# Splitting the 512-column matmuls of the second MLP's second product into two of 256 columns

## The chip, the cores and the metric

The kernel runs on one core of one Trainium2 chip. The metric is the device time of one execution in microseconds (us), as the median of several runs; smaller is better. Engines are named as in the profile: PE is TensorE's matmul, PEld its weight load (the stationary operand of a matmul), DVE is VectorE, ACT is ScalarE, POOL is GpSimd, and SP issues most DMAs.

## What is computed

Three layers follow one another. Linear attention with an RMS norm makes `x` of 2304 tokens by 512. A first MLP with three input products, a maximum over them and an output product follows. The second MLP, a mixture of four dense experts, takes more than half of the time, and the change is in it:

```python
def _moe2_ref(x, domain_probs, w1, w2):
    p = domain_probs / (domain_probs.sum(-1, keepdims=True) + 1e-09)
    out = np.zeros((2304, 512), dtype=np.float32)
    for e in range(4):
        h = np.maximum(x @ w1[e], 0.0)          # 512 -> 1024
        out += p[:, e:e + 1] * (h @ w2[e])      # 1024 -> 512
    return out
```

`h @ w2[e]` is the second product of the second MLP.

## The kernel before, in words

All matmuls of the MLPs use operands of type fp32r. To keep more precision, a value is split into a high part and a low remainder, and a product of two values is made of three matmuls: high by high, high by low, low by high. They are summed in a PSUM bank of 512 fp32 columns.

The second MLP works in rounds. A round (loop at L1029) is one expert `e` (4), one superblock `sb` of 768 tokens (3) and one `pr` (4), which stands for two blocks of 128 hidden channels: 48 rounds in all. Each round has two kinds of matmuls, written to different banks:

- The first product of this round. `seven` (L591) is called seven times (`k` = 0 to 6, through `product`, L586). Each call issues 6 matmuls of 384 columns (L597): seven products stand for the eight of a 2 by 2 block multiplication, by sums and differences of operands formed ahead. They alternate between two banks, 7 and 6. After each, ACT and DVE read the bank, form the hidden values and split them into high and low parts (L619 to L625, and `hide`, L603).
- The second product of the round before. `second` (L728) is a generator: for each of six blocks of 128 tokens (`ORDER`, banks 3, 4, 5, 0, 1, 2), for two blocks of hidden channels `a`, and for the three high and low pairs, it issues one matmul (L736). Its stationary operand is a 128 by 128 piece of the hidden values `h`, its moving operand is a row block of `w2` of 128 by 512. That makes 36 matmuls of 512 columns in a round and 1728 in 48 rounds.

The order on PE is written by hand. After the `k`-th product of the round the loop takes `AFTER[k]` matmuls from the generator (`AFTER` at L461, its sum is 36), so that PE has work while ACT and DVE read out the product's bank. When the last matmul of a token block in the last `pr` has been issued, the generator yields the block's number, and `store` (L746) scales the bank by the expert's probability, adds it up and writes it to memory. After the last round the loop at L1061 runs the 36 remaining matmuls with nothing between them.

The first MLP is run in the same manner, with matmuls of 384 columns only (L260, L424, L597, L704), before the first matmul of L736 at 376.2 us.

Of the kernel before, what the change touches and what calls it, by code (L numbers as in the profile page):

```python
# [21 lines left out]
def tile_attn_moe_moe2(  # L22
# [23 lines left out]
    nc = tc.nc  # L46
# [4 lines left out]
    P = 128  # L51
# [5 lines left out]
    TPB = T // P  # L57
# [21 lines left out]
    banks = [ps.tile([P, 512], F32, name=f"bank{n}") for n in range(8)]  # L79
# [372 lines left out]
    NPR = NEF // 2  # L452
# [5 lines left out]
    BANKS = "AXAXAAX"  # L458
    BEGIN = (0, 1, 3)

    AFTER = (5, 5, 5, 5, 7, 5, 4)  # L461


    FILL = [(0, 2, 1, 2, 2, 5, 2, 2), (0, 2, 1, 2, 2, 5, 2, 2), (0, 2, 1, 2, 2, 5, 2, 2)]
# [29 lines left out]
    def w_slot(pr):  # L494
        t, at = (wl, 0) if pr == 0 else (wr[0], (pr - 1) * 11 * DM)
        first = [part(t, at + i * 7 * 2 * P, 7 * 2 * P) for i in range(2)]
        at += 7 * DM
        second = [
            [part(wl, 11 * DM, DM) if (pr, a, i) == (3, 1, 1) else part(t, at + (2 * a + i) * DM, DM) for i in range(2)]
            for a in range(2)  # L500
        ]
        return first, second
# [76 lines left out]
    def y_split(k):  # L579
        hi, lo = y_op(k)  # L580
        src = y_part(Y_AT[k]).rearrange("p (c t) -> p c t", c=2)
        nc.scalar.activation(out=hi, in_=src, func=AF.Copy)  # L582
        low(lo, src, hi)
# [25 lines left out]
    def h_of(n):  # L609


        s = (2, 5) if n % 2 else (0, 1)
        return {(0, 0): h_unit(s[0]), (1, 0): h_unit(s[1]), (0, 1): h_unit(3), (1, 1): h_unit(4)}
# [114 lines left out]
    def second(n, pr):  # L728

        h = h_of(n + NPAIRS + 1)  # L730
        _, w = w_slot(pr)
        for i in ORDER:
            for a in range(2):
                for m, (hi, wi) in enumerate(((0, 0), (0, 1), (1, 0))):
                    last = (a, m) == (1, 2)
                    nc.tensor.matmul(  # L736
                        banks[i], h[a, i // TPB][hi][:, i % TPB * P : (i % TPB + 1) * P], w[a][wi],
                        start=(pr == 0 and a == 0 and m == 0), stop=(pr == NPR - 1 and last),
                    )
                    yield i if last else None  # L740

    def o_load(sb):
        for i in ORDER:
# [37 lines left out]
    with tc.manual_schedule():  # L781
# [75 lines left out]
        for st in steps:  # L857
# [33 lines left out]
            elif kind == "A":  # L891
                i, j, f = at
# [136 lines left out]
        for n, (e, sb, pr) in enumerate(rounds):  # L1029
# [3 lines left out]
            if before is not None:  # L1033
                e0, sb0, pr0 = before
                rest = second(n - 1, pr0)
            for k in range(7):
                product(pr, k)
                after_product(n, k)
                if n == 0:
                    lag_at(7 * len(units) + k)  # L1040
                    go(fill, FILL_18[1 + k])
                    for i in SPLIT.get((0, k), ()):
                        y_split(i)
                for _ in range(AFTER[k]):
                    ended = next(rest, None)
# [15 lines left out]
        for i in second(n, pr):  # L1061
            if i is not None:
                store(e, sb, i)
# [32 lines left out]
```

## Time and profile before

| what | value |
| --- | --- |
| median of 3 runs | 1129.35 us (1128.74 to 1131.17) |
| profiled execution, its time from first to last instruction (span) | 1126.5 us |
| PE busy | 1105.5 us, 98% of the span |
| PEld busy | 1014.4 us, 90% |
| DVE, ACT, POOL busy | 662.0, 429.0 and 156.4 us |

The profile records one execution. It gives no time of its own for that execution beside the span; the median of the runs is 2.85 us above the span. In the timeline a row is a merged run of equal instructions: its start, its length from the first start to the last end, engine, line, operation, the output and inputs by name, the shapes and the count. Matmuls overlap at their ends: the length of one matmul in a row is longer than the distance from its start to the next one's start. The distance between starts is the rate at which PE goes on, and it is got from the starts of two rows and the count of matmuls from the one to the other.

### The profile page before, as it was taken

What the parts mean: (1) busy time and instruction counts of PE and PEld (TensorE: products, weight loads), DVE (VectorE), ACT (ScalarE), POOL (GpSimd) and SP (SyncE); (2) the same over time, 40 slices, a digit from 0 to 9 for tenths busy, and PEclk for the clock granted to TensorE, in tenths of its full rate; (3) what the DMA queues carried; (4) which work ended last, traced back from release to release, by engine and by line L of the source; (5) the groups of instructions that cost most, each with busy time, mean ns of one, the idle gap of its engine ahead of it and who ended that gap; (6) DMA issues with size and microseconds to landing.
All of it is one profiled execution on the core that took longest, in us unless ns stands there. A gap on an engine that the chain in (4) does not pass through costs nothing.

```text
span 1126.5 us, 15294 instructions
## 1 busy us (share of the span) xinstructions
PE 1105.5 (98%) x6020; PEld 1014.4 (90%) x6020; DVE 662.0 (59%) x1023; ACT 429.0 (38%) x774; POOL 156.4 (14%) x164
## 2 busy tenths in 40 slices
PE   7899999999999999999999999999999999999998
PEld 7789999999999989988889988898989988898987
DVE  3889985667667672445745454764535575544523
ACT  2553233434344453343624242442324353323321
POOL 1346632420101100012100002110000220000000
PEclk8999999999999999999999999999999999999999
DMA  9955555332511503032230406240120625040111
GB/s 268 289 152 172 151 180 197 128 113 83 160 38 38 187 19 112 1 131 75 88 138 19 150 1 211 70 171 35 66 103 26 200 75 187 1 168 2 57 55 57
DMA packets 89257, 123.20 MB, mean 109 GB/s; under 512 B 11616, under 2 KB 57696, under 8 KB 89184
## 3 DMA queue, kind: packets, MB, share of 16 engines
q1 hardware_dynamic: 88480, 121.89, 33.8%
q8 instruction: 47, 0.77, 0.3%
q10 hardware_dynamic: 704, 0.33, 0.1%
q14 instruction: 26, 0.21, 0.1%
HBM read 87.59 MB, written 34.60 MB: 108 GB/s over the span
## 4 chain that ended last, share of the span: by engine, by line
PE 83%; DVE 9%; DMA 2%; issue 2%; ACT 1%; SPq 1%; POOL 1%; DVEq 0%; ACTq 0%; POOLq 0%
PE bank L597 42%; PE bank L736 36%; PE bank L704 3%; PE bank L424 1%; DVE cv_a L233 1%; DMA w_da<-cv_a 1%; DMA v<-in_v_dram 1%; DVE rb L508 1%; DVE fa L405 1%; DVE cv_a L236 1%; DMA k<-in_k_dram 1%; DVE cv_a L232 1%; DVE wr L210 1%; POOL cv_a L225 0%; SPq L138 0%
## 5 line engine op out<-in xcount | busy, mean ns | idle before, releaser
L736 PE MATMUL bank<-wr,hr 128*128 128x512 f32 x720 | 197.3, 393 | 0.0
L622 DVE TENSOR_TENSOR fa<-bank,fa 128x384 f32<-128x384 f32 x144 | 80.2, 557 | 181.3 <-ACT fa L619 99.6
L538 POOL TENSOR_TENSOR w1s<-w1s 128x256 f32<-128x256 f32 x96 | 82.7, 881 | 634.2 <-DMA w1s<-in_moe_w_dram 559.1
L597 PE MATMUL bank<-xr,wr 128*128 128x384 f32 x756 | 153.5, 338 | 0.0
L736 PEld LDWEIGHTS bank<-wr,hr 128*128 128x128 f32 x720 | 133.6, 188 | 17.8
L597 PEld LDWEIGHTS bank<-xr,wr 128*128 128x128 f32 x756 | 135.9, 188 | 9.8
L619 ACT ACTIVATE fa<-bank 128x384 f32<-128x384 f32 x144 | 70.5, 489 | 188.8 <-PE bank L597 188.0
L597 PE MATMUL bank<-rb,wr 128*128 128x384 f32 x696 | 141.3, 337 | 0.5 <-DVE hr L605 0.5
L597 PEld LDWEIGHTS bank<-rb,wr 128*128 128x128 f32 x696 | 125.1, 188 | 10.4 <-DVE hr L605 0.8
L736 PE MATMUL bank<-wl,hr 128*128 128x512 f32 x360 | 102.8, 394 | 0.0
L736 PE MATMUL bank<-wr,xr 128*128 128x512 f32 x288 | 93.9, 394 | 0.0
L597 PE MATMUL bank<-rb,wl 128*128 128x384 f32 x384 | 77.8, 339 | 0.1
L736 PEld LDWEIGHTS bank<-wl,hr 128*128 128x128 f32 x360 | 66.8, 188 | 8.6
L597 PEld LDWEIGHTS bank<-rb,wl 128*128 128x128 f32 x384 | 68.2, 188 | 4.2 <-DVE fa L680 0.4
L736 PE MATMUL bank<-wr,rb 128*128 128x512 f32 x216 | 69.0, 393 | 0.0
L605 DVE SCALAR_TENSOR_TENSOR hr<-fa,hr 128x384 fp32r<-128x384 f32 x72 | 43.4, 603 | 42.6 <-ACT hr L604 42.6
L604 ACT ACTIVATE hr<-fa 128x384 fp32r<-128x384 f32 x72 | 37.8, 525 | 78.8 <-DVE fa L622 78.8
L604 ACT ACTIVATE xr<-fa 128x384 fp32r<-128x384 f32 x48 | 25.2, 526 | 98.7 <-DVE fa L622 98.7
L736 PEld LDWEIGHTS bank<-wr,xr 128*128 128x128 f32 x288 | 53.9, 188 | 7.9
L680 DVE TENSOR_TENSOR fa<-bank,fa 128x384 f32<-128x384 f32 x54 | 29.9, 554 | 51.6 <-ACT fa L677 36.3
L508 DVE TENSOR_TENSOR rb<-fa,rb 128x768 fp32r<-128x768 f32 (+1 forms) x45 | 42.5, 946 | 28.8 <-ACT rb L582 28.1
L573 DVE TENSOR_TENSOR fa<-fa 128x768 f32<-128x768 f32 x56 | 54.4, 984 | 0.3
(175 smaller groups left out, 1759.7 us busy)
## 6 DMA issues: line engine op xcount, KB each, us to landing
fa<-y_d SPq DMA_DIRECT2D x24, 768.0 KB, 6.0
stage_a<-in_moe_w_dram SPq DMA_DIRECT2D x18, 512.0 KB, 3.9
o_d<-fa SPq DMA_DIRECT2D x36, 256.0 KB, 3.7
fa<-o_d SPq DMA_DIRECT2D x36, 256.0 KB, 5.3
w2s<-in_moe_w_dram SPq DMA_DIRECT2D x32, 256.0 KB, 3.7
w1s<-in_moe_w_dram SPq DMA_DIRECT2D x30, 256.0 KB, 2.9
w_da<-cv_a SPq DMA_DIRECT2D x18, 256.0 KB, 4.6
w1s<-w_da SPq DMA_DIRECT2D x18, 256.0 KB, 3.3
```

Of the source, the lines that this page charges most:

```text
L210: eng.tensor_tensor(out=w[:, 1, :], in0=t, in1=f32(w[:, 0, :]), op=ALU.subtract)
L508: nc.vector.tensor_tensor(out=lo, in0=src, in1=f32(hi), op=ALU.subtract)
L538: eng.tensor_tensor(out=st[o], in0=st[a], in1=st[b], op=ALU.subtract)
L573: eng.tensor_tensor(out=y_part(o), in0=y_part(a), in1=y_part(b), op=op)
L597: nc.tensor.matmul(out, w[wi][:, c * P : (c + 1) * P], y[yi][:, c, :], start=(i == 0 and k in BEGIN), stop=(i == 5), skip_group_check=k no ...
L604: nc.scalar.activation(out=h[0], in_=src, func=AF.Relu)
L605: nc.vector.scalar_tensor_tensor(out=h[1], in0=src, scalar=0.0, in1=f32(h[0]), op0=ALU.max, op1=ALU.subtract)
L619: nc.scalar.activation(out=s[k // 2], in_=a, func=AF.Copy)
L622: nc.vector.tensor_tensor(out=t, in0=x, in1=t, op=ALU.add)
L680: nc.vector.tensor_tensor(out=mx[done] if i == 0 else t, in0=x, in1=t, op=ALU.add)
L704: nc.tensor.matmul(bank[:, :T], w[:, wi, c * P : (c + 1) * P], h[a, blk][hi], start=((blk == 1 or p == 0) and a == 0 and n == 0), stop=((b ...
L736: nc.tensor.matmul(banks[i], h[a, i // TPB][hi][:, i % TPB * P : (i % TPB + 1) * P], w[a][wi], start=(pr == 0 and a == 0 and m == 0), stop ...
```

## The change

Each matmul of `second` is issued as two, over columns 0 to 255 and 256 to 511 of the same bank, with the same stationary operand and one half each of the moving operand. The start flag is on the first half alone, and the group check is skipped, since two matmuls write one bank's group. The generator now yields 72 times for a round, and the numbers in `AFTER` are doubled, so that the halves stand where the whole ones stood.

```diff
-    AFTER = (5, 5, 5, 5, 7, 5, 4)
+    AFTER = (10, 10, 10, 10, 14, 10, 8)
...
-                    nc.tensor.matmul(
-                        banks[i], h[a, i // TPB][hi][:, i % TPB * P : (i % TPB + 1) * P], w[a][wi],
-                        start=(pr == 0 and a == 0 and m == 0), stop=(pr == NPR - 1 and last),
-                    )
-                    yield i if last else None
+                    for half in range(2):
+                        cols = slice(half * 2 * P, (half + 1) * 2 * P)
+                        nc.tensor.matmul(
+                            banks[i][:, cols], h[a, i // TPB][hi][:, i % TPB * P : (i % TPB + 1) * P], w[a][wi][:, cols],
+                            start=(pr == 0 and a == 0 and m == 0 and half == 0), stop=(pr == NPR - 1 and last),
+                            skip_group_check=True,
+                        )
+                        yield i if last and half else None
```

The order on PE in the middle of a round, before. Here `bank_73` and `bank_72` are the two banks of the first product, `bank_66` to `bank_71` the six of the second; `hr`, `xr` hold hidden values, `wl`, `wr` the weights. Names in brackets are the engines waited for.

```order
L597 MATMUL bank_73<-rb,wr 128x384 [waits DVE_49]
L597 MATMUL bank_73<-rb,wr 128x384 x5
L736 MATMUL bank_69<-wl,hr 128x512 [waits Activation_49]
L736 MATMUL bank_69<-wl,hr 128x512 x4
L597 MATMUL bank_72<-rb,wr 128x384 [waits DVE_49]
L597 MATMUL bank_72<-rb,wr 128x384 x5
L736 MATMUL bank_69<-wl,hr 128x512
L736 MATMUL bank_70<-wl,hr 128x512 x4
```

The same place on PE after the change:

```order
L597 MATMUL bank_73<-rb,wr 128x384 [waits DVE_49]
L597 MATMUL bank_73<-rb,wr 128x384 x5
L738 MATMUL bank_69<-wl,hr 128x256 [waits Activation_49]
L738 MATMUL bank_69<-wl,hr 128x256 x9
L597 MATMUL bank_72<-rb,wr 128x384 [waits DVE_49]
L597 MATMUL bank_72<-rb,wr 128x384 x5
L738 MATMUL bank_69<-wl,hr 128x256 x2
L738 MATMUL bank_70<-wl,hr 128x256 x8
```

Five matmuls of 512 columns became ten of 256 between the same two first products, with the same waits in front. On ACT, DVE, POOL and SP the rows and their waits are the same before and after, but for line numbers.

The end of PE's order, before: the last token block of the last round.

```order
L736 MATMUL bank_68<-wr,rb 128x512 x3
L736 MATMUL bank_68<-wr,xr 128x512
L736 MATMUL bank_68<-wl,xr 128x512
L736 MATMUL bank_68<-wr,xr 128x512
L1091 UNCONDITIONAL_BRANCH
```

The end of PE's order after the change:

```order
L738 MATMUL bank_68<-wr,rb 128x256 x6
L738 MATMUL bank_68<-wr,xr 128x256 x2
L738 MATMUL bank_68<-wl,xr 128x256 x2
L738 MATMUL bank_68<-wr,xr 128x256 x2
L1094 UNCONDITIONAL_BRANCH
```

Six matmuls became twelve, and what reads the bank afterwards is unchanged.

## Rows read from the trace of the kernel before

**Rows 1.** The page: span, and each engine's busy time, share and instructions.

```profile
span 1126.5 us, 15294 instructions
...
PE 1105.5 (98%) x6020; PEld 1014.4 (90%) x6020; DVE 662.0 (59%) x1023; ACT 429.0 (38%) x774; POOL 156.4 (14%) x164
```

**Rows 2.** Busy time by stretch: us, engines' busy us (instructions), granted clock, DMA.

```profile
420.00:1100.00 680.00, 680.00 (x3377) 611.85 (x3376) 351.21 (x514) 250.44 (x442) 40.95 (x48) 1.00 0.26 89
1100.00:1126.50 26.50, 22.32 (x106) 18.97 (x104) 8.41 (x13) 3.05 (x6) 0.00 (x0) 0.98 0.18 61
```

**Rows 3.** The page: the chain that ended last, by engine and by line.

```profile
PE 83%; DVE 9%; DMA 2%; issue 2%; ACT 1%; SPq 1%; POOL 1%; DVEq 0%; ACTq 0%; POOLq 0%
PE bank L597 42%; PE bank L736 36%; PE bank L704 3%; PE bank L424 1%; DVE cv_a L233 1%; DMA w_da<-cv_a 1%; DMA v<-in_v_dram 1%; DVE rb L508 1%; DVE fa L405 1%; DVE cv_a L236 1%; DMA k<-in_k_dram 1%; DVE cv_a L232 1%; DVE wr L210 1%; POOL cv_a L225 0%; SPq L138 0%
```

**Rows 4.** Groups by shape, line 736: count, busy us, mean ns of one, idle before.

```profile
L736 PE MATMUL bank<-wr,hr 128*128 128x512 f32 x720 | 197.3, 393 | 0.0
L736 PEld LDWEIGHTS bank<-wr,hr 128*128 128x128 f32 x720 | 133.6, 188 | 17.8
L736 PE MATMUL bank<-wl,hr 128*128 128x512 f32 x360 | 102.8, 394 | 0.0
L736 PE MATMUL bank<-wr,xr 128*128 128x512 f32 x288 | 93.9, 394 | 0.0
L736 PE MATMUL bank<-wr,rb 128*128 128x512 f32 x216 | 69.0, 393 | 0.0
L736 PE MATMUL bank<-wl,xr 128*128 128x512 f32 x144 | 49.2, 396 | 0.0
```

**Rows 5.** Timeline of the end, 512-column matmuls alone: first and last row, last read-out.

```profile
1113.13 1.79 PE L736 MATMUL bank<-wr,hr 128*128 128x512 f32 x7
...
1121.92 0.40 PE L736 MATMUL bank<-wr,xr 128*128 128x512 f32 x1
1122.35 0.75 DVE L753 SCALAR_TENSOR_TENSOR fa<-bank,p_all,fa 128x512 f32<-128x512 f32 x1 [0.64 <-PE bank L736]
```

**Rows 6.** Timeline of PE, first MLP, 384-column matmuls alone: first and last row.

```profile
334.07 1.22 PE L597 MATMUL bank<-op,ts 128*128 128x384 f32 x6
...
344.23 1.07 PE L597 MATMUL bank<-op,ts 128*128 128x384 f32 x5
```

**Rows 7.** Timeline of PE: first rows of two rounds, one after the other.

```profile
1066.66 1.23 PE L597 MATMUL bank<-rb,wr 128*128 128x384 f32 x6
...
1082.41 1.21 PE L597 MATMUL bank<-rb,wr 128*128 128x384 f32 x6
```

**Rows 8.** Timeline: two weight loads after a wait, at two places; matmuls at the second.

```profile
373.44 0.30 PEld L597 LDWEIGHTS bank<-xr,wl 128*128 128x128 f32 x2 [0.17 <-DVE xr L508]
...
194.28 0.30 PEld L597 LDWEIGHTS bank<-rb,wl 128*128 128x128 f32 x2
...
194.03 0.70 PE L597 MATMUL bank<-rb,wl 128*128 128x384 f32 x3
```

**Rows 9.** Timeline of the attention stage: matmuls of plain fp32 over 128 columns, loads.

```profile
49.16 3.61 PE L332 MATMUL bank<-kvb,qT 128*128 128x128 f32 x30
49.37 3.21 PEld L332 LDWEIGHTS bank<-kvb,qT 128*128 128x128 f32 x28
```

## The prediction, made before the changed kernel was run

> **What bounds the kernel now.** I read the page first. PE is busy for 1105.5 of 1126.5 us, and no other engine reaches two thirds of that, weight loads aside [rows 1]. A busy share is only an average, so I looked at the stretch the change is in. From 420 to 1100 us PE is busy for 680.00 of 680.00 us at a granted clock of 1.00, the higher of its two levels (2.4 GHz); DVE is busy for 351 us of it and ACT for 250 [rows 2]. The chain of waits confirms it: 42% of the span goes through the matmuls of L597 and 36% through those of L736 [rows 3]. The groups of L736 count 720 + 360 + 288 + 216 + 144 = 1728 matmuls, with 0.0 us of idle time before them [rows 4]. So in the 48 rounds each nanosecond that PE gains or loses per matmul of L736 reaches the end, 1728 times: 1 ns is 1.73 us, or 0.15%.
>
> A matmul's length in a row (393 ns [rows 4]) says nothing of the rate, since matmuls overlap at their ends. The rate is the distance between starts:
>
> - 512 columns: at the end only these run. From the first at 1113.13 to the 39th at 1121.92 us lie 38 distances [rows 5]: 8.79 / 38 = 231.3 ns.
> - 384 columns: in the first MLP only these run. From 334.07 to 344.23 us lie 58 distances (counts of the 14 rows from the first on, up to the last: 58) [rows 6]: 10.16 / 58 = 175.2 ns.
> - Check: a round of 36 and 42 of them should take 36 x 0.2313 + 42 x 0.1752 = 15.69 us; two rounds start 15.75 us apart [rows 7]. The 0.06 us left are the round's waits between the groups.
>
> **The change, part by part.**
>
> *Removed and added.* In 48 rounds 1728 matmuls of 512 columns go, and 3456 of 256 come. As many columns stream through the array as before, so any cost comes with the number of instructions. No row shows a matmul of this type over 256 columns. I take its price from the two sizes that rows show. From 384 to 512 columns the distance grows by 231.3 - 175.2 = 56.1 ns for 128 columns; a straight line leaves 175.2 - 3 x 56.1 = 6.9 ns for a matmul without columns, and gives 175.2 - 56.1 = 119.1 ns at 256. Two halves take 238.2 ns in place of 231.3, which is 6.9 ns more, and 1728 x 6.9 ns = 11.9 us.
>
> *Bounds of this price.* Below: if the distance goes with the columns alone, a half takes 231.3 / 2 = 115.7 ns by the size that is split (0.0 us in all), or 175.2 x 2/3 = 116.8 ns by the other size (+2.3 ns a pair, +4.0 us). Lower still, the attention's matmuls of plain fp32 over 128 columns go at the pace of their loads, (3.21 - 0.19) / 27 = 111.9 ns [rows 9]. That is the fastest that full loads of 128 by 128 follow one another in a stream here, and two of these would take 223.8 ns: -7.5 ns a pair, -13.0 us. Above: if an estimate of one column per tick of 2.4 GHz holds, 512 columns stream in 213.3 ns and 384 in 160.0, and the remainder of a matmul is 18.0 or 15.2 ns. If all of that remainder comes once per matmul, whatever its size, the pair costs 15.2 to 18.0 ns more: +26.3 to +31.1 us. I take the straight line, because the remainder is seen to grow with the columns (15.2 to 18.0), which neither bound has.
>
> By the Trainium skill ("TensorE: Matmul & The Clock Gate", section "Back-to-back issue gap") matmuls at the full clock start N / 2.4 + 2.5 ns apart, so a split would cost 2.5 ns for each pair, an estimate of +4.3 us in all. The trace disagrees with that formula in size: it gives 215.8 ns for 512 columns where rows 5 give 231.3.
>
> *Weight loads.* Each matmul carries its own load of the stationary operand: PE and PEld both count 6020 [rows 1]. The two halves use the same operand, and the order shows them as two whole matmuls, so I count 1728 more loads. One load is 188 ns long [rows 4], longer than a half. But that is a length, not a rate: where loads stood behind a wait, two took 0.30 us, so the second began 0.30 - 0.19 = 0.11 us after the first [rows 8]. At the second place of that group this happened while a matmul of 384 columns streamed: three matmuls in 0.70 us, with 0.34 us for the last one's length (six in 1.22 us [rows 6] leave 1.22 - 5 x 0.175 = 0.34), are (0.70 - 0.34) / 2 = 0.18 us apart, hardly more than the usual 0.175. So a load needs 0.11 us of its unit, beside the stream, and fits under a half of 119 ns with some 8 ns to spare. I cost the loads at nothing; the cover is the half that streams, and the point at which it is gone is a load of more than 119 ns.
>
> *Order, waits, other engines.* The doubled `AFTER` puts the halves where the whole matmuls stood, ACT, DVE, POOL and SP keep their orders, and no wait is added. Between two first products PE has 10 x 119.1 ns = 1191 in place of 5 x 231.3 = 1157 ns, so ACT and DVE get more time to read out a bank, not less. They do not pace a stage in which PE has no idle time [rows 2], so this buys nothing. The read-out at the end starts 0.43 us after the last matmul's start (1122.35 - 1121.92 [rows 5]); the end of the program moves with that matmul.
>
> **Sum.** +11.9 us on PE, nothing hidden, nothing else. The profiled execution would go from 1126.5 to 1138.4 us. The median of the runs stands 2.85 us above that span, and I take that part as unchanged: 1129.35 + 11.9 = **1141.3 us**, 1.1% slower.
>
> **Rivals.**
>
> 1. *The remainder is paid per matmul.* The upper bound above, +20 to +31 us, 1149 to 1161 us. For it speaks that the remainders of the two sizes are close (15.2 and 18.0 ns); against it that they do grow.
> 2. *The remainder goes with the columns.* 0 to +4 us, 1129 to 1133 us: about no change. For it speaks that 231.3 / 175.2 = 1.320 is near 512 / 384 = 1.333; against it the 6.9 ns that the line leaves.
> 3. *Faster.* If a good part of what a 512-column matmul loses per column is lost because it streams long (a stall that only builds up in the second half of a stream), halves run at the pace of the loads, 111.9 ns: -13.0 us, 1116 us. It decides from the point where a half takes less than 115.7 ns. Rows 9 show such a pace, but for another type of operand, and the shorter of the two sizes here loses more per column, not less (175.2 / 384 = 0.456 ns against 0.452).
> 4. *The loads come out from under the stream.* If the loads take turns with the stream, at 0.11 us each 1728 loads cost up to 190 us: 1319 us. If the load only slows a little when the stream beside it never pauses, say to 130 ns, a pair takes 260 ns, and the sum is +49.6 us, 1179 us. Against the first speak rows 8, where the stream went on during a load; nothing speaks against the second but that a load's 0.11 us was the same at a place with a stream and a place without.
>
> The Trainium skill has the rule of rival 4 in the same page, Part 3, section "The mechanism": loads overlap matmuls in flight only where they go to other row groups, which matmuls on all 128 rows never do. By that rule the loads would lie bare already now; the rows of this trace speak against it.
>
> That the change doesn't do what it says is excluded by the order: 3456 matmuls of 128x256 stand on PE.
>
> **How the numbers follow.** About 0.2%, or 2.3 us, is what a measurement of this kernel can tell from no change. Chances: forecast (a half of 118 to 121 ns, 1137 to 1148 us) 0.60; rival 1 0.14; rival 2 0.12, half of it within 2.3 us; rival 3 0.05; rival 4 0.09. Slower by over 0.2%: 0.60 + 0.14 + 0.06 + 0.09 = 0.89. Within 0.2%: 0.06. Faster: 0.05. The range leaves out rival 3, rival 4 and most of the part of rival 2 that is no change, 0.20 together: from 1131 us to the end of rival 1, 1161 us.
>
> **What would show it.** In the profile after, the line of the halves should count 3456 with no idle time before, PE should be busy without a gap in the rounds at a clock of 1.00, the stretch at the end should have 77 distances of about 119 ns, and rounds should start 36 x 6.9 ns = 0.25 us further apart, at 16.0 us. Distances of 122 ns and more speak for rival 1, below 116 for rivals 2 or 3. Loads that follow one another 2 or 3 ns after a matmul's start and still end the distance, at more than 121 ns, speak for rival 4. Idle time on PE in the rounds, or a clock below 1.00, would mean that I missed a mechanism altogether.

## The result and the profile after

The changed kernel takes 1143.27 us (median of 4 runs, 1141.77 to 1145.25); the kernel before, run beside it, takes 1130.26 us (1128.74 to 1131.56). The ratio is 1.0111, with a 95% interval of 1.0099 to 1.0123: 13.0 us slower, where +11.9 us was forecast. The profiled execution has a span of 1140.0 us, 13.5 more than before.

The page of the changed kernel, span and engines, then the chain that ended last by engine and line:

```profile
span 1140.0 us, 18750 instructions
...
PE 1117.2 (98%) x7748; PEld 1101.6 (97%) x7748; DVE 662.3 (58%) x1023; ACT 429.0 (38%) x774; POOL 155.5 (14%) x164
...
PE 83%; DVE 9%; DMA 3%; issue 2%; ACT 1%; POOL 1%; SPq 0%; DVEq 0%; ACTq 0%; POOLq 0%
PE bank L597 41%; PE bank L738 36%; PE bank L704 3%; PE bank L424 1%; DMA v<-in_v_dram 1%; DMA w_da<-cv_a 1%; DVE cv_a L233 1%; DVE rb L508 1%; DVE cv_a L236 1%; DVE fa L405 1%; DVE wr L210 1%; DVE cv_a L232 1%; DMA stage_o<-in_moe_w_out_dram 1%; PE bank L332 0%; DVE ss L346 0%
```

Against [rows 1], PE and PEld each have 7748 - 6020 = 1728 instructions more, so every half has its own weight load; DVE, ACT and POOL count and work as before. In its main parts the chain is that of [rows 3], with L738 where L736 was.

Busy time of one stretch in the rounds of the changed kernel (us, then PE, PEld, DVE, ACT, POOL, the granted clock and DMA):

```profile
425.00:1110.00 685.00, 685.00 (x4899) 685.00 (x4898) 348.48 (x509) 248.33 (x438) 40.08 (x48) 1.00 0.26 88
```

PE is busy without a gap at a clock of 1.00, as in [rows 2]. What is new is PEld: it too is busy for all of it, where it had pauses before (611.85 of 680).

Groups of the new line by shape (the largest pair), and below them PE's timeline: the first rows of two rounds, then of the end the first two rows and the last:

```profile
L738 PE MATMUL bank<-wr,hr 128*128 128x256 f32 x1440 | 201.7, 281 | 0.0
L738 PEld LDWEIGHTS bank<-wr,hr 128*128 128x128 f32 x1440 | 191.7, 188 | 0.0
```

```profile
1079.13 1.22 PE L597 MATMUL bank<-rb,wr 128*128 128x384 f32 x6
...
1095.12 1.21 PE L597 MATMUL bank<-rb,wr 128*128 128x384 f32 x6
...
1126.09 0.40 PE L738 MATMUL bank<-wr,xr 128*128 128x256 f32 x2
1126.33 1.82 PE L738 MATMUL bank<-wr,hr 128*128 128x256 f32 x14
...
1135.33 0.40 PE L738 MATMUL bank<-wr,xr 128*128 128x256 f32 x2
```

A load is still 188 ns long [rows 4], in a stream whose matmuls start every 119 ns: a load's length is not the pace at which loads follow one another. From 1126.09 to 1135.33 lie 78 halves: 9.24 us / 78 = 118.5 ns (forecast 119.1, against 231.3 for a whole one in [rows 5]). Rounds start 15.99 us apart, 0.24 more than in [rows 7] (forecast 0.25).

To price one edit over all 48 rounds I use the stretch from the first to the last start of a second-product matmul, which the view of one line gives. For the kernel before and for the changed one (count, shortest, median and longest in ns, first and last start in us):

```profile
L736 PE MATMUL bank<-wl,hr x360: 387/393/402, 376.2 to 1117.5; 128*128 128x512 f32 x180
...
L736 PE MATMUL bank<-wr,xr x288: 390/393/398, 401.0 to 1121.9; 128*128 128x512 f32 x144
```

```profile
L738 PE MATMUL bank<-wl,hr x720: 276/283/290, 378.5 to 1131.0; 128*128 128x256 f32 x180
...
L738 PE MATMUL bank<-wr,xr x576: 274/281/291, 403.7 to 1135.5; 128*128 128x256 f32 x192
```

Before: 1121.9 - 376.2 = 745.7 us. After: 1135.5 - 378.5 = 757.0 us. That is 11.3 us, or 6.5 ns for each of 1728 matmuls. The other 2.3 us of the span's 13.5 lie before the rounds: the first of these matmuls starts at 378.5 in place of 376.2. Nothing of the change stands there. In the nine traces of this case that start lies between 376.2 and 379.6 us and does not grow with the number of matmuls, so I read it as the spread of single executions. The one trace of the kernel before has the earliest of the nine, so the traces alone do not show that it is spread.

### The profile page after: what moved, and what is told of

Same layout as the page of the kernel before. It is cut to its first block, busy times and chain, and to the rows that moved or that the text cites. A ratio compares the mean times of both kernels' runs of the same rounds, so it can differ in the third digit from the quotient of the medians.

```text
span 1140.0 us, 18750 instructions
## 1 busy us (share of the span) xinstructions
PE 1117.2 (98%) x7748; PEld 1101.6 (97%) x7748; DVE 662.3 (58%) x1023; ACT 429.0 (38%) x774; POOL 155.5 (14%) x164
## 4 chain that ended last, share of the span: by engine, by line
PE 83%; DVE 9%; DMA 3%; issue 2%; ACT 1%; POOL 1%; SPq 0%; DVEq 0%; ACTq 0%; POOLq 0%
PE bank L597 41%; PE bank L738 36%; PE bank L704 3%; PE bank L424 1%; DMA v<-in_v_dram 1%; DMA w_da<-cv_a 1%; DVE cv_a L233 1%; DVE rb L508 1%; DVE cv_a L236 1%; DVE fa L405 1%; DVE wr L210 1%; DVE cv_a L232 1%; DMA stage_o<-in_moe_w_out_dram 1%; PE bank L332 0%; DVE ss L346 0%
## 5 line engine op out<-in xcount | busy, mean ns | idle before, releaser
L738 PE MATMUL bank<-wr,hr 128*128 128x256 f32 x1440 | 201.7, 281 | 0.0
L738 PEld LDWEIGHTS bank<-wr,hr 128*128 128x128 f32 x1440 | 191.7, 188 | 0.0
L597 PE MATMUL bank<-xr,wr 128*128 128x384 f32 x756 | 153.6, 338 | 0.0
L597 PE MATMUL bank<-rb,wr 128*128 128x384 f32 x696 | 141.5, 338 | 0.5 <-DVE hr L605 0.5
L597 PEld LDWEIGHTS bank<-xr,wr 128*128 128x128 f32 x756 | 128.6, 188 | 0.1
L597 PEld LDWEIGHTS bank<-rb,wr 128*128 128x128 f32 x696 | 117.9, 188 | 1.0 <-DVE hr L605 0.8
L738 PE MATMUL bank<-wl,hr 128*128 128x256 f32 x720 | 105.5, 283 | 0.0
L738 PEld LDWEIGHTS bank<-wl,hr 128*128 128x128 f32 x720 | 98.6, 190 | 0.0
L738 PE MATMUL bank<-wr,xr 128*128 128x256 f32 x576 | 95.7, 281 | 0.0
L738 PEld LDWEIGHTS bank<-wr,xr 128*128 128x128 f32 x576 | 82.6, 188 | 0.0
L597 PE MATMUL bank<-rb,wl 128*128 128x384 f32 x384 | 77.8, 339 | 0.0
L738 PE MATMUL bank<-wr,rb 128*128 128x256 f32 x432 | 70.7, 282 | 0.0
L597 PEld LDWEIGHTS bank<-rb,wl 128*128 128x128 f32 x384 | 66.0, 188 | 1.1 <-DVE fa L680 0.4
L738 PEld LDWEIGHTS bank<-wr,rb 128*128 128x128 f32 x432 | 62.5, 189 | 0.0
```

Of the source, the lines that this page charges most:

```text
L597: nc.tensor.matmul(out, w[wi][:, c * P : (c + 1) * P], y[yi][:, c, :], start=(i == 0 and k in BEGIN), stop=(i == 5), skip_group_check=k no ...
L738: nc.tensor.matmul(banks[i][:, cols], h[a, i // TPB][hi][:, i % TPB * P : (i % TPB + 1) * P], w[a][wi][:, cols], start=(pr == 0 and a == 0 ...
```

## The experiments

Two things had to be told apart: what an extra matmul costs of itself, and how near the weight loads are to setting the pace. The theory is the prediction's: a matmul over N columns takes 6.9 ns + 0.438 ns x N, but never less than the pace of the loads, some 111 ns, since one load runs beside one matmul's stream. Rival A is new: the load of an operand that is already in the array costs nothing. Rival B is a form of the prediction's rival 4: the 119 ns of a half are already the pace of the loads. Edits are shown against the kernel before, but for the half-outer and half-dose runs, whose edits are shown against the changed kernel.

### Four quarters, and uneven pieces

```diff
-                    nc.tensor.matmul(
-                        banks[i], h[a, i // TPB][hi][:, i % TPB * P : (i % TPB + 1) * P], w[a][wi],
-                        start=(pr == 0 and a == 0 and m == 0), stop=(pr == NPR - 1 and last),
-                    )
-                    yield i if last else None
+                    for piece, (c0, c1) in enumerate([(0, 128), (128, 256), (256, 384), (384, 512)]):
+                        nc.tensor.matmul(
+                            banks[i][:, c0:c1], h[a, i // TPB][hi][:, i % TPB * P : (i % TPB + 1) * P], w[a][wi][:, c0:c1],
+                            start=(pr == 0 and a == 0 and m == 0 and piece == 0), stop=(pr == NPR - 1 and last),
+                            skip_group_check=True,
+                        )
+                        yield i if last and piece == 3 else None
```

`AFTER` is multiplied by the number of pieces. The uneven runs have the list `[(0, 288), (288, 512)]`, `[(0, 384), (384, 512)]` or `[(0, 272), (272, 512)]`, with `piece == 1`.

Quarters, expected: 

> Each matmul of the second product over 512 columns as four over 128. Theory (a matmul of this type takes 6.9 ns + 0.438 ns per column, and never less than its weight load's pace of about 111 ns, since one load fits under one matmul): a quarter streams in 63 ns by the line, so the load sets the pace: 4 x 111 = 444 ns in place of 231.4, +213 ns x 1728 = +368 us, about 1498 us. Rival A (the load of the operand that is already in the array costs nothing): 4 x 63 = 252 ns, +36 us, about 1166 us. Rival B (the 119 ns of a half is already the pace of the loads): 4 x 119 = 476 ns, +423 us, about 1553 us.

Measured: 1501.9 us against 1132.16, ratio 1.3277 (1.325 to 1.3303), +369.7 us where the theory had +368. The groups, the end of the timeline of PE and of PEld, and the view of the line:

```profile
L737 PEld LDWEIGHTS bank<-wr,hr 128*128 128x128 f32 x2880 | 345.1, 192 | 0.0
L737 PE MATMUL bank<-wr,hr 128*128 128x128 f32 x2880 | 345.1, 272 | 0.0
```

```profile
1495.19 0.61 PE L737 MATMUL bank<-wr,xr 128*128 128x128 f32 x4
1495.64 0.61 PE L737 MATMUL bank<-wl,xr 128*128 128x128 f32 x4
1496.09 0.61 PE L737 MATMUL bank<-wr,xr 128*128 128x128 f32 x4
...
1495.58 0.53 PEld L737 LDWEIGHTS bank<-wl,xr 128*128 128x128 f32 x4
1496.03 0.53 PEld L737 LDWEIGHTS bank<-wr,xr 128*128 128x128 f32 x4
```

```profile
L737 PE MATMUL bank<-wl,hr x1440: 221/275/280, 379.5 to 1487.9; 128*128 128x128 f32 x180
...
L737 PE MATMUL bank<-wr,xr x1152: 220/274/278, 416.5 to 1496.4; 128*128 128x128 f32 x192
```

Four quarters start every 0.45 us, and four loads start every 0.45 us: 112 ns each. Over the whole stretch (1496.4 - 379.5 = 1116.9 us) a matmul's four pieces take 371.2 us / 1728 = 214.8 ns more than before, so a quarter takes (231.3 + 214.8) / 4 = 111.5 ns. The line alone would give 63 ns. Half as many columns as in a half save only 7 ns: from here on the loads are the bound. Rival A falls, since all four pieces use the same operand, and rival B falls, since the loads can go faster than 119 ns.

288 and 224 columns, expected: 

> Each matmul as two of 288 and 224 columns in place of 256 and 256. Theory: 133.1 ns and, as the line's 105.1 ns is below the load's pace, 111 ns: 244 ns, +12.7 ns x 1728 = +22 us against 512 columns, about 1152 us, some 10 us above the even split. Rival A (loads of the same operand cost nothing): 238.2 ns like the even split, about 1142 us. Rival B (a load's pace is 119 ns): 133.1 + 119 = 252 ns, +36 us, about 1166 us.

384 and 128 columns, expected: 

> Each matmul as two of 384 and 128 columns. Theory: 175.2 + 111 = 286 ns, +55 ns x 1728 = +95 us, about 1225 us. Rival A: 175.2 + 63 = 238.2 ns as with the even split, about 1142 us. Rival B: 175.2 + 119 = 294 ns, +108 us, about 1239 us.

Measured: 1154.71 us, ratio 1.0201 (1.0186 to 1.0216), and 1224.76 us, ratio 1.0822 (1.0804 to 1.084), both against 1132.16 us. That is +22.5 and +92.6 us where the theory had +22 and +95. The view of the line with 288 and 224:

```profile
L737 PE MATMUL bank<-wl,hr x720: 261/282/308, 379.6 to 1144.1; 128*128 128x288 f32 x180
...
L737 PE MATMUL bank<-wr,xr x576: 261/282/305, 405.2 to 1148.8; 128*128 128x288 f32 x96, 128*128 128x224 f32 x96
```

The view of the line with 384 and 128:

```profile
L737 PE MATMUL bank<-wl,hr x720: 220/280/397, 379.5 to 1213.7; 128*128 128x384 f32 x180
...
L737 PE MATMUL bank<-wr,xr x576: 218/280/392, 407.3 to 1219.2; 128*128 128x384 f32 x96, 128*128 128x128 f32 x96
```

Two pieces of timeline with 384 and 128, PEld and then PE (a merged row carries the shape of its first matmul):

```profile
1217.44 0.87 PEld L737 LDWEIGHTS bank<-wr,rb 128*128 128x128 f32 x6
1218.30 0.30 PEld L737 LDWEIGHTS bank<-wr,xr 128*128 128x128 f32 x2
...
1217.50 1.02 PE L737 MATMUL bank<-wr,rb 128*128 128x384 f32 x6
1218.36 0.45 PE L737 MATMUL bank<-wr,xr 128*128 128x384 f32 x2
```

Three pairs take 1218.36 - 1217.50 = 0.86 us, 287 ns a pair, which is 175 for 384 columns and 112 for a piece that should stream in 63. The two loads of a pair start 0.30 - 0.19 = 0.11 us apart: the load that starts with the short piece needs longer than the piece, and the next matmul's stream waits for it. From the stretches, the pair costs 54.4 ns more than a whole matmul with 384 and 128 (839.7 us) and 13.6 ns more with 288 and 224 (769.2 us). Taking off the line's time of the long piece, the short one takes 231.3 + 54.4 - 175.2 = 110.5 and 231.3 + 13.6 - 133.1 = 111.8 ns. With the quarters' 111.5 that is one floor from three experiments.

A fixed pace at which PE could start any pair of a load and a matmul, whatever the size of the load, would look the same in these three runs. A row of the kernel before speaks against it. In the attention stage 40 matmuls with loads of 64 columns take 1.82 us, less than 46 ns each:

```profile
45.27 1.82 PE L282 MATMUL bank<-v,k 128*64 128x64 f32 x40
```

They are matmuls of plain fp32 that write by turns to two halves of the partitions, so the row is a hint and no proof: no run changed the width of a load in the second MLP.

The same number of matmuls, columns and loads as in the even split costs 10 to 80 us more by the place of the cut alone.

### The knee: 272 and 240 columns

> Each matmul as two of 272 and 240 columns. Theory: 126.1 + 112.1 ns, both just above the load's pace of 111 ns, so the sum is that of the even split, 238.2 ns: +12 us, a ratio of 1.010. If the load's cover is already short at 240 columns (matmuls vary by some ns about their mean, and a short one is held up by its load): up to 3 ns more for each pair, +17 us, a ratio of 1.015.

Measured: 1140.12 us against 1131.24, ratio 1.0081 (1.0067 to 1.0094), +8.9 us. The view of the line:

```profile
L737 PE MATMUL bank<-wl,hr x720: 269/281/293, 377.3 to 1128.1; 128*128 128x272 f32 x180
...
L737 PE MATMUL bank<-wr,xr x576: 269/281/295, 402.4 to 1132.6; 128*128 128x272 f32 x96, 128*128 128x240 f32 x96
```

The stretch is 755.3 us, which is 5.6 ns more for each pair. By the subtraction used above the short piece takes 231.3 + 5.6 - 126.1 = 110.8 ns. So at 240 columns the load adds nothing to the line's 112.1 ns, but the floor lies so near that no room is left; at 224, in the run above, the piece takes 111.8 ns where the line has 105.1, and the load shows. The theory's number was missed slightly to the other side: the interval ends below 1.010, so this cut is a little cheaper than the line says, by 1.3 ns a pair. Why is open; the line through two sizes is no better than that.

### The order of the halves

```diff
-            for a in range(2):
-                for m, (hi, wi) in enumerate(((0, 0), (0, 1), (1, 0))):
-                    last = (a, m) == (1, 2)
-                    for half in range(2):
-                        cols = slice(half * 2 * P, (half + 1) * 2 * P)
+            for half in range(2):
+                cols = slice(half * 2 * P, (half + 1) * 2 * P)
+                for a in range(2):
+                    for m, (hi, wi) in enumerate(((0, 0), (0, 1), (1, 0))):
+                        last = (a, m) == (1, 2)
```

> The halves of 256 columns in another order: for each token block first the six matmuls over columns 0 to 255, then the six over 256 to 511, so that two halves with the same stationary operand no longer follow one another. Theory: each matmul has its own load anyway, hidden under a half, so nothing changes against the split: about 1143 us, halves 119 ns apart. Rival A (the second half's load is skipped or shortened because its operand is in the array): the distance of halves grows by what a real load adds, and the time goes over 1148 us.

Measured: 1142.05 us against 1132.16, ratio 1.0092 (1.0077 to 1.0107); its interval overlaps that of the change. The view of the line gives 1135.8 - 379.2 = 756.6 us, 6.3 ns for each split matmul against 6.5:

```profile
L738 PE MATMUL bank<-wl,hr x720: 276/283/290, 379.2 to 1131.4; 128*128 128x256 f32 x180
...
L738 PE MATMUL bank<-wr,xr x576: 274/280/285, 403.0 to 1135.8; 128*128 128x256 f32 x192
```

That the two halves share a stationary operand neither saves nor costs anything that shows here. The edit thins out the repeats and does not end them: the first two of the three high and low pairs use the same high part of `h`, so of a block's 12 matmuls 8 have the operand of the one just before in the changed kernel, and 4 here. The quarters, which take 1501.9 us where rival A gives 1166, are the stronger evidence that the load is done for each matmul.

### Half the dose

```diff
                     for half in range(2):
-                        cols = slice(half * 2 * P, (half + 1) * 2 * P)
+                        if i < TPB and half:
+                            yield i if last else None
+                            continue
+                        cols = slice(half * 2 * P, (half + 1) * 2 * P) if i >= TPB else slice(0, 4 * P)
```

> Only the token blocks in banks 3, 4 and 5 are split, so 864 of the 1728 matmuls. Theory (each extra matmul costs its own 6.5 to 6.9 ns on PE): 864 x 6.7 ns = +5.8 us on the kernel before, a ratio of 1.005. If the cost were not that of the matmuls (a change in the first stages, or one wait that moves), half the split would not cost half: 0 or the whole +11 to +13 us (1.010 to 1.011).

Measured: 1137.49 us against 1131.24, ratio 1.0055 (1.0042 to 1.0069), +6.3 us. The interval holds 1.005 and neither 1 nor 1.010. The stretch of its line (377.4 to 1128.7, 751.3 us) is 5.6 us longer, 6.5 ns for each of 864 split matmuls:

```profile
L741 PE MATMUL bank<-wl,hr x612: 276/283/398, 377.4 to 1124.4; 128*128 128x256 f32 x126, 128*128 128x512 f32 x27
...
L741 PE MATMUL bank<-wr,xr x288: 389/393/404, 402.4 to 1128.7; 128*128 128x512 f32 x144
```

### The other product: 384 columns as two of 192

```diff
-                nc.tensor.matmul(
-                    out, w[wi][:, c * P : (c + 1) * P], y[yi][:, c, :],
-                    start=(i == 0 and k in BEGIN), stop=(i == 5), skip_group_check=k not in BEGIN,
-                )
+                for half in range(2 if parts else 1):
+                    cols = slice(half * T // 2, (half + 1) * T // 2) if parts else slice(0, T)
+                    nc.tensor.matmul(
+                        out[:, cols], w[wi][:, c * P : (c + 1) * P], y[yi][:, c, cols],
+                        start=(i == 0 and half == 0 and k in BEGIN), stop=(i == 5), skip_group_check=True,
+                    )
```

`parts` is true for the calls from `product` alone, the second MLP's.

> The kernel before, but the 2016 matmuls of the second MLP's first product over 384 columns are done as two over 192 each. Theory: by the line a piece streams in 91 ns, so the load's pace of 111 ns sets it: 2 x 111 - 175.2 = +47 ns x 2016 = +95 us, about 1226 us. Rival A (loads of the same operand cost nothing): 6.9 ns x 2016 = +14 us, about 1145 us. If ACT and DVE, not PE, paced this stage, less than +95 us.

Measured: 1226.09 us against 1131.24, ratio 1.084 (1.0825 to 1.0855), +94.9 us. Its groups by shape and the view of the second product's line, which is whole here:

```profile
L599 PEld LDWEIGHTS bank<-rb,wr 128*128 128x128 f32 x1344 | 169.5, 191 | 9.7 <-DVE hr L607 0.3
L599 PE MATMUL bank<-rb,wr 128*128 128x192 f32 x1296 | 159.9, 272 | 0.0
```

```profile
L738 PE MATMUL bank<-wl,hr x360: 387/396/426, 378.7 to 1213.8; 128*128 128x512 f32 x180
...
L738 PE MATMUL bank<-wr,xr x288: 390/394/419, 406.7 to 1218.2; 128*128 128x512 f32 x144
```

The stretch is 1218.2 - 378.7 = 839.5 us, 93.8 us more. Of the 2016 matmuls 1968 start inside it, since the 42 of the first round and six of the second come before it. That is 47.7 ns for each, where the floor says 2 x 111 - 175.2 = 47. So the floor holds for another line, other operands and other waits, and PE, not ACT or DVE, paces the stage.

## Why the prediction was right

- *PE is the bound, and every nanosecond per matmul arrives.* Right. PE has no gap in the rounds, ACT and DVE kept their work, and half the dose cost half.
- *The price.* 6.9 ns for each split matmul was forecast, 11.9 us in all. The stretch shows 6.5 ns, 11.3 us, and the runs +13.0 us with an interval of 1.0099 to 1.0123, that is 11.2 to 13.9 us. The straight line through 384 and 512 columns gave 119.1 ns for 256; the end of the timeline has 118.5. Both bounds (rivals 1 and 2) are off: if the remainder came once per matmul, a half would take 122 to 125 ns, and if the time went with the columns alone, 115.7. The reason given for the straight line was weak. The remainder grows with the columns under the lower bound too: by the same estimate, time that goes with the columns alone leaves 13.5 ns at 384 columns and 18.0 at 512. Two sizes cannot show that the line is straight, and 272 with 240 columns cost 1.3 ns a pair less than it says; that it met 256 columns within 0.6 ns is in part luck.
- *Loads hidden, with 8 ns to spare.* Right, and this was the step with most to lose. The floor of 111 ns, taken before from two loads behind a wait [rows 8], is 110.5 to 111.8 ns in three experiments. Of the 8 ns to spare 7 were there (118.5 against 111.5). The cover is gone at 224 columns and just enough at 240. In the changed kernel loads are in progress all the time, and it still costs nothing: busy time of PEld is no measure of how near the loads are to being the bound.
- *Rival 3, faster.* The pace it counted on, 111.9 ns from matmuls of plain fp32 [rows 9], exists, but as the floor of the loads. A half's own stream takes longer.
- *Rival 4, loads taking turns with the stream.* Excluded by the quarters: a load at 111 ns and a stream of 63 one after the other would be 174 ns, and the quarters start 111.5 ns apart. The milder form, a half of more than 121 ns, is excluded by the 118.5 ns measured. The Trainium skill's rule that loads overlap only with matmuls of other row groups ("TensorE: Matmul & The Clock Gate", Part 3, section "The mechanism") does not hold in these rounds, where all matmuls and loads use all 128 rows; the same section also lets a load into a background weight buffer go ahead of matmuls, which agrees with the 111.5 ns. The Trainium skill's price for a load, columns / 1.2 GHz (the same page, section "LDWEIGHTS (loading the stationary operand)"), gives an estimate of 107 ns for 128 columns, near the 111 measured.
- *The sum.* 1141.3 us forecast, 1143.27 measured, 2.0 us more. Of these, 0.9 us is the kernel before: run beside the changed one it took 1130.26 us, and the sum starts from 1129.35. The other 1.1 us is the difference, 13.0 in place of 11.9, and the interval of the ratio is 2.7 us wide. In the profile the rounds took 0.6 us less than forecast, and 2.3 us more lie before them. That an extra matmul of the second product delays the stages ahead of it is unlikely: in five of the six other runs that split this product the medians grew by 0.7 to 1.5 us less than the stretch, and in the sixth, half the dose, by 0.7 us more.

What the 6.5 ns consist of, and why the stream takes 0.438 ns a column, more than one tick of 2.4 GHz (0.417), stays open: no run took the load away from under a matmul.

## What to carry to other kernels

On an engine without idle time an instruction that seems free costs its own start: read the distance between starts at two sizes, and a line through them prices a third to about 1 ns. Then look for the floor that the line doesn't show, here the pace of the weight loads, which belongs to each matmul even when its stationary operand was used just before. For matmuls of this kind the moving side should stay above some 240 columns, and where a cut must be made, an even or nearly even one is the cheap one: 384 and 128 cost 93 us where 256 and 256 cost 13.

## What was not expected

- 272 and 240 columns cost 5.6 ns a pair, less than the line and no more than 256 and 256 (6.5). A price good to 1 ns a matmul needs a measurement at the size itself, not the line.
- In the profile a matmul that waits for its load starts early and looks long. Beside the short piece, the piece of 384 columns reaches a length of 397 ns, where it has 338 in the groups of L597 in the kernel before; a quarter and a piece of 192 columns both show 272. So lengths hide a bound by the loads as well as a rate, and only the distances show it.
